# A decode step with a 4096-wide attention window: the first key loads over two queues, 256-byte key buffers, and a finer last cut

## The chip, the cores and the metric

The kernel runs on one core of one Trainium2 chip. The metric is the device time of one execution in microseconds (us); less is better. Names used below: PE is TensorE (matmuls; PEld its weight loads), DVE is VectorE, ACT is ScalarE, POOL is GpSimd, SP is SyncE, which only issues transfers here. PSUM is the memory that matmuls write to, SBUF the memory that the other engines and the transfers work on. A "q" behind an engine's name in the profile means its instruction queue (ACTq, SPq); q1 and q10 are the DMA queues that SP and ACT fill.

## The reference

One token (batch 1, one position, width 512) passes an attention over the last 4096 cached positions with 32 heads of 128, and beside it a small MLP block; the two are multiplied and added to the input.

```python
def reference(A_x, A_k_cache, A_v_cache, A_wq, A_wo, B_x, B_w1, B_w2, B_w3, B_w4):
    # attention on xn: W = 4096, 32 heads, Dh = 128
    q = (x @ wq).reshape(1, 1, 32, 128)
    k, v = k_cache[:, :, Sk - W:, :], v_cache[:, :, Sk - W:, :]
    p = softmax(einsum("bhqd,bhkd->bhqk", q, k) * Dh ** -0.5)
    s = einsum("bhqk,bhkd->bhqd", p, v) ... @ wo
    # block B on xn, with S = 1: the shifts leave only zeros, so hs = zeros @ w2
    x1 = x + hs
    g = silu(x1 + gelu(layernorm(x1) @ w3) @ w4)
    return A_x + s * g          # xn = layernorm(A_x) goes into both
```

The window's keys and values are 33.5 MB each in bf16, which with wq, wo and the block's weights makes the 79 MB that the core has to read.

## The kernel before

**Tiling.** The 32 heads are worked in eight groups of four (G = 4). A group's keys, or values, are one tile of 128 partitions by 128 chunks by 128 numbers in bf16 (4 MB, 32 KB per partition); each head has 32 of the partitions. Three key buffers (pool "k", K_BUFS = 3) and two value buffers (pool "v", V_BUFS = 2) are reused in turn. In this text K0 to K7 and V0 to V7 are the eight groups' keys and values.

**Scores.** The chunks of a group are shared between two ways. The first nd(g) chunks (64 in groups 0 and 7, else 80) go through DVE in four parts (k_vector): a product of keys and the query (L321, tile prod) and a sum along the 128 numbers (L323, tile S). The rest goes through PE in batches (k_turn, k_scores): transposes of two chunks at a time (L339), a copy by ACT from PSUM (L342, tile kt), and matmuls with the query (L350, tile sT). sm_own and sm_max bring both together and take the row maximum (L359, L364, L366); sm_turn and sm_exp spread the maximum over the partitions and take the exponentials (L372 to L388, tile pT).

**Values.** v_wide multiplies values with pT in matmuls over four chunks (L427, tile ov), v_turn and v_add fold the result (L444, L450), v_out divides (L471). Of the last group, the last 32 chunks go chunk by chunk through v_part (L461), into the same sum.

**Stages.** The main loop runs s = 0 to 9 with LAG = 2: stage s scores group s, takes the exponentials of group s - 1 and weighs the values of group s - 2. Inside it, the order on PE, DVE and ACT is the one written in the code (a manual schedule). What comes before the loop (layer norms, the query, the MLP block up to g_row, masks) is put in order by the scheduler, and so are its places among the first stage's instructions.

**Queues.** ACT issues x_bf, x_row and wq; every other load is issued by SP in program order through load(): w2, w3, w4 (two transfers), then K0 in two halves, K1, K2, V0, K3, V1 and so on. A load that reuses a buffer waits on SP until the engines are done with it, and what is behind it on SP waits too. V0's buffer lies in the memory of the pool "wts" (wq, w2, w3, w4 and a few tiles), which is closed in stage 2; V0's load waits for that pool's last readers, among them the matmuls into h2_ps (L155) that read hr.

**The end.** V7 comes in three pieces, cut at chunks 64 and 96 (cuts = (0, 64, 96, CP)); after it come two loads of the last four heads' rows of wo (wo_rows). When V7's last piece has landed, PE runs its 32 matmuls, DVE divides, PE multiplies with wo_rows (y_head), DVE multiplies with g_row and adds x, and SP writes the output.

**Memory.** The pool "k" is the first in SBUF; ahead of it lie 16,384 bytes of scratch and four constants of 32 bytes, so the key buffers begin at byte 16,512 of each partition. The value buffers begin at 160,000 and 192,768.

The lines that set the loads, and the names the change touches:

```python
kn = load_kv(k_pool, A_k_cache, s, (0, 64, CP) if s == 0 else (0, CP)) if s < NG else None   # L534
neg_half = const.tile([P, 33], FP32, name="neg_half")     # L121, only column 0 is read (L178)
bv = small.tile([P, P], FP32, name="bv")                  # L277
cuts = (0, 64, 96, CP)                                    # L526
```

Of the kernel before, what the change touches and what calls it, by code (L numbers as in the profile page):

```python
# [8 lines left out]
P = 128  # L9
BF16 = mybir.dt.bfloat16  # L10
FP32 = mybir.dt.float32
ACT = mybir.ActivationFunctionType
ALU = mybir.AluOpType
# [6 lines left out]
LAG = 2  # L20
# [6 lines left out]
def kernel(  # L27
# [14 lines left out]
    nc = tc.nc  # L42
# [3 lines left out]
    _, H, Sk, Dh = A_k_cache.shape  # L46
# [5 lines left out]
    CP = G * W // P  # L52
# [4 lines left out]
    scale = float(Dh) ** -0.5  # L57


    k_pool = ctx.enter_context(tc.tile_pool(name="k", bufs=K_BUFS))  # L60
    kt_pool = ctx.enter_context(tc.tile_pool(name="kt", bufs=4))
    prod_pool = ctx.enter_context(tc.tile_pool(name="prod", bufs=1))
    const = ctx.enter_context(tc.tile_pool(name="const", bufs=1))
    small = ctx.enter_context(tc.tile_pool(name="small", bufs=1))
# [7 lines left out]
    wts_guard = tc.tile_pool(name="wts", bufs=1)  # L72
    wts = wts_guard.__enter__()

    def load(dst, src):
        return tc.keep_in_program_order(nc.sync.dma_start(out=dst, in_=src))  # L76

    x_bf = small.tile([P, KC], BF16, name="x_bf")
    nc.scalar.dma_start(out=x_bf[:], in_=A_x.rearrange("a b (p c) -> p (a b c)", p=P))
# [5 lines left out]
                        in_=A_wq.rearrange("(a b c) n -> b a (c n)", a=4, c=KC))  # L85
# [6 lines left out]
    load(w4_sb[0:96, 10, :], B_w4[10 * P:F, :])  # L92


    def load_kv(pool, cache, g, cuts=(0, CP)):
        t = pool.tile([P, CP, Dh], BF16, tag="kv", name="kv")
        src = cache[0, G * g:G * g + G, W0:, :].rearrange("a (b c) d -> b a (c d)", b=PB)
        dst = t[:].rearrange("p c d -> p (c d)")
        for c0, c1 in zip(cuts, cuts[1:]):
            load(dst[:, c0 * Dh:c1 * Dh], src[:, :, c0 * Dh:c1 * Dh])  # L100
        return t

    ident_bf = const.tile([P, P], BF16, name="ident_bf")
    make_identity(nc, ident_bf[:])
# [13 lines left out]
    nc.vector.tensor_copy(out=sel[:], in_=ident_bf[:, 0:P:32].unsqueeze(1).to_broadcast([P, PB, G]))  # L118
    ind = const.tile([P, 1], FP32, name="ind")
    nc.vector.tensor_reduce(out=ind[:], in_=ident_f[:, 0:P:32], axis=AX.X, op=ALU.max)  # L120
    neg_half = const.tile([P, 33], FP32, name="neg_half")  # L121
    nc.vector.memset(neg_half[:], -0.5)


# [27 lines left out]
    def rows_add(ps, col, w, last):  # L152
        k = col.shape[0]
        for j in range(KC):
            nc.tensor.matmul(ps[32 * j:32 * j + 1, :], lhsT=col, rhs=w[0:k, j * P:(j + 1) * P],  # L155
                             start=False, stop=last, skip_group_check=True)
# [60 lines left out]
    for b in range(2):  # L217
# [5 lines left out]
        for t in range(2):  # L223
            rows = slice(64 * t, 64 * t + 64)
            nc.scalar.copy(out=q_pair[rows, 4 * b:4 * b + 4, :, G * t:G * t + G].rearrange("p g l a -> p g a l"),
                           in_=qt_ps[rows].bitcast(BF16).rearrange("p g (a m l) -> p g a m l", a=G, l=2)[:, :, :, 0, :])
# [14 lines left out]
    xn_row = small.tile([P, P], FP32, name="xn_row")  # L241
# [26 lines left out]
    for i, (col, w) in enumerate(terms):  # L268
# [5 lines left out]
    h2_ps = ps_misc.tile([P, P], FP32, tag="misc", name="h2_ps")  # L274
    rows_open(h2_ps)
    rows_add(h2_ps, ind, hr, True)
    bv = small.tile([P, P], FP32, name="bv")  # L277
    nc.vector.tensor_tensor(out=bv[:], in0=xn_row[:], in1=h2_ps[:], op=ALU.add)
    g_row = small.tile([P, P], FP32, name="g_row")
    nc.scalar.activation(out=g_row[:], in_=bv[:], func=ACT.Silu)  # L280


    make_masks(16)
# [13 lines left out]
                            op=ALU.max)  # L297
    par_t = const.tile([1 + G, PB, G], FP32, name="par_t")
    nc.vector.tensor_scalar(out=par_t[:],
                            in0=ident_f[0:1 + G, 1:1 + G].unsqueeze(1).to_broadcast([1 + G, PB, G]),  # L300
# [26 lines left out]
    def batches(g):  # L327
        n, m = nd(g), CP - nd(g)
        k = -(-m // 8)
        edges = [n + 2 * (m // 2 * i // k) for i in range(k + 1)]  # L330
        return list(zip(edges, edges[1:]))
# [12 lines left out]
    def k_scores(g, b):  # L344
        kt = kts.pop(b)
        c0, c1 = batches(g)[b]
        for i in range((c1 - c0) // 2):
            c = c0 + 2 * i - nd(g)
            for l in range(2):
                nc.tensor.matmul(st[g]["sT"][:, c:c + 2, :].rearrange("p c a -> p (c a)"),  # L350
                                 lhsT=kt[:, i, l::2], rhs=q_pair[:, g, l, :], start=(l == 0), stop=(l == 1))
# [55 lines left out]
    def load_wo(i):  # L407
        h0, n = blocks[i]
        load(wo_blk[i], A_wo[h0 * P:(h0 + n) * P, :].rearrange("(p t) n -> p t n", p=P))
# [4 lines left out]
    def load_rows(h, n):  # L414
        load(wo_rows[:, h - h_part:h - h_part + n, :],
             A_wo[h * P:(h + n) * P, :].rearrange("(h p) n -> p h n", p=P))
# [41 lines left out]
    def v_part(g, v, c0, c1):  # L458
        s = st[g]
        for c in range(c0, c1):  # L460
            nc.tensor.matmul(s["oT"][:], lhsT=v[:, c, :], rhs=s["pT"][:, c, :], start=False,  # L461
                             stop=(c == CP - 1), skip_group_check=True)
# [60 lines left out]
        rows_add(y_ps, o_blk[3][:, h - h_part:h - h_part + 1], wo_row(h), h == H - 1)  # L523

    NG = H // G
    cuts = (0, 64, 96, CP)  # L526
    region = tc.manual_schedule(engines={mybir.EngineType.PE, mybir.EngineType.DVE,
                                         mybir.EngineType.Activation})
    region.__enter__()
# [1 line left out]
    for s in range(NG + LAG):  # L531
        h = s - LAG
        last = h == NG - 1
        kn = load_kv(k_pool, A_k_cache, s, (0, 64, CP) if s == 0 else (0, CP)) if s < NG else None  # L534
        if s == LAG:
            wts_guard.__exit__(None, None, None)
            v_pool = ctx.enter_context(tc.tile_pool(name="v", bufs=V_BUFS))
            wo_blk[2] = v_pool.tile([P, 4, D], BF16, tag="wo_4", bufs=1, name="wo_4")
            wo_rows = v_pool.tile([P, H - h_part, D], BF16, tag="wo_rows", bufs=1, name="wo_rows")
        if last:  # L540
            v = load_kv(v_pool, A_v_cache, h, cuts)
            for r in (H - G, H - 2):
                load_rows(r, 2)
        elif h >= 0:
            v = load_kv(v_pool, A_v_cache, h)
        if h == 3:
            wo_24 = k_pool.tile([P, 32, D], BF16, tag="kv", name="wo_24")
            wo_blk[0], wo_blk[1] = wo_24[:, 0:16, :], wo_24[:, 16:24, :]
            load_wo(0)
        if h == 5:  # L550
            load_wo(1)
            load_wo(2)

        if s < NG:
            nb = len(batches(s))

            def keys(b0, b1):
                for b in range(b0, b1):
                    k_turn(s, kn, b)
                    if b > 0:  # L560
                        k_scores(s, b - 1)

            k_open(s)
            k_vector(s, kn, 0)
            keys(0, 2)
            if s == 7:
                v_turn(h - 1)
                v_add(h - 1)
                v_out(h - 1)
            elif s > 1:  # L570
                sm_den(s - 2)
                sm_rden(s - 2)
            elif s == 1:
                sm_max(0)
            k_vector(s, kn, 1)
            keys(2, 4)
            if s == 7:
                sm_den(h)
                sm_rden(h)
                keys(4, nb - 2)  # L580
                sm_turn(s - 1)
                keys(nb - 2, nb)
            else:
                if s > 0:
                    sm_turn(s - 1)
                keys(4, nb)
            k_scores(s, nb - 1)
            sm_own(s)
            if s == 7:
                k_vector(s, kn, 2)  # L590
                v_wide(h, v)
                sm_exp(s - 1)
                v_turn(h)
                y_open()
                k_vector(s, kn, 3)
                v_add(h)
                v_out(h)
                ox_spread(1)
                sm_max(s)
                continue  # L600
            if s > 0:
                sm_exp(s - 1)
            if h > 0:
                v_turn(h - 1)
            k_vector(s, kn, 2)
            if h >= 0:
                v_wide(h, v)
            if h > 0:
                v_add(h - 1)
                v_out(h - 1)  # L610
            if s == 6:
                ox_spread(0)
            k_vector(s, kn, 3)
            if s == 6:
                ox_pick(0)
            if s > 0:
                sm_max(s)
        elif s == NG:
            ox_pick(1)
            sm_turn(NG - 1)  # L620
            sm_exp(NG - 1)
            y_wide(1, False)
            sm_den(NG - 2)
            sm_rden(NG - 2)
            y_wide(0, False)
            warm(3)
            v_wide(h, v)
            sm_den(NG - 1)
            sm_rden(NG - 1)
            v_turn(h)  # L630
            v_add(h)
            v_out(h)
            ox_spread(2)
        else:
            v_open(h)
            warm(3)
            v_wide(h, v, cuts[1], last=False)
            ox_pick(2)
            y_wide(2, True)
            nc.scalar.copy(out=y_sum[:], in_=yr[0][:].rearrange("p j n -> p (j n)"))  # L640
            v_wide(h, v, cuts[2], cuts[1])
            v_turn(h)
            v_add(h)
            rows_add(y_ps, ind, y_sum, False)
            v_part(h, v, cuts[2], CP)
            v_out(h)
            for r in range(H - G, H):
                y_head(r)
# [36 lines left out]
```

## Time and profile before

| What | us |
|---|---|
| median of 3 runs (lowest, highest) | 193.31 (193.19, 193.39) |
| the profiled execution's own time | 193.34 |
| its span, first to last instruction | 191.2 |
| DVE busy | 150.9 (79%) |
| PE busy | 116.4 (61%) |
| ACT busy | 89.2 (47%) |
| DMA, mean over the span | 413 GB/s, 79.02 MB |
| one 4 MB key load, median from issue to landing | 31.3 |
| first key product on DVE starts | 26.09 |
| last piece of V7 landed | 186.33 |

The profile is of one execution. The span is shorter than the device time, which also counts what lies around the first and the last instruction. A row of the groups reads: line, engine, operation, tiles written and read with their shapes, count, busy time, mean time of one, and what ended the idle time ahead of it. A row of the timeline begins with the start time and the duration in us and ends, where the engine had been idle, with the idle time and what ended it in square brackets. A row of busy times by stretches has the stretch and its length, then busy us (and instructions) of PE, PEld, DVE, ACT and POOL, then PE's granted clock as a share of full speed, the mean busy share of the 16 DMA engines, and GB/s. A DMA queue's row has the number of packets, MB, and their time as a share of 16 engines.

The chain of work that ended last is, by the page, 46% DVE, 43% DMA, 5% PE and 3% ACT.

### The profile page before, as it was taken

Reading aid. Unit: us, or ns where it says so; the run is one execution under the profiler, and the core shown is the slowest. Engines: PE = TensorE matmul, PEld = TensorE weight load, DVE = VectorE, ACT = ScalarE, POOL = GpSimd, SP = SyncE. Lnnn points to the kernel's source line nnn. Section 1 sums busy time; section 2 is a strip of 40 time slices with the busy share of each in tenths; the row PEclk is TensorE's granted clock in tenths of the full one; section 3 lists DMA queues with packets and bytes.
Section 4 is the critical chain, followed back from the end, with each engine's and each line's share of the span. In section 5 each row is a group of like instructions: output and inputs, shape, how many; then the busy total and the mean of one; then the engine's idle time right before and its main releaser. Section 6 shows DMA issues by size and latency. Waiting matters only on the chain.

```text
span 191.2 us, 2839 instructions
## 1 busy us (share of the span) xinstructions
PE 116.4 (61%) x1159; PEld 74.2 (39%) x1159; DVE 150.9 (79%) x175; ACT 89.2 (47%) x191; POOL 2.3 (1%) x11
## 2 busy tenths in 40 slices
PE   1653754989825368256845772680888189739762
PEld 0430222767614334143334441540763077313322
DVE  1660159979999999999999999999999999980111
ACT  2001370888794076427464564542475148733120
POOL 2110000000000000000000000000000000000000
PEclk9999695555755557955695588557567858975998
DMA  6999999999999999999999999999999998999990
GB/s 211 447 430 404 431 418 439 439 439 437 432 434 439 432 429 432 432 439 432 422 432 432 418 422 418 452 439 435 439 432 434 435 432 372 471 425 405 420 371 32
DMA packets 4572, 79.02 MB, mean 413 GB/s; under 512 B 624, under 2 KB 1232, under 8 KB 1488
## 3 DMA queue, kind: packets, MB, share of 16 engines
q1 hardware_dynamic: 4264, 74.65, 91.6%
q10 hardware_dynamic: 296, 4.20, 5.1%
q8 instruction: 9, 0.15, 0.3%
q14 instruction: 3, 0.02, 0.0%
HBM read 78.84 MB, written 0.00 MB: 412 GB/s over the span
## 4 chain that ended last, share of the span: by engine, by line
DVE 46%; DMA 43%; PE 5%; ACT 3%; issue 1%; SPq 1%; ACTq 0%; DVEq 0%
DMA kv<-in_A_k_cache_dram 31%; DVE S L323 28%; DVE prod L321 15%; DMA kv<-in_A_v_cache_dram 10%; ACT kt L342 3%; DMA x_bf<-in_A_x_dram 2%; PE pt L339 2%; PE ov L427 1%; DVE m L366 1%; DVE S L364 1%; SPq L76 1%; PE sT L350 1%; DVE mx L374 1%; PE oT L461 1%; PE ot_ps L444 0%
## 5 line engine op out<-in xcount | busy, mean ns | idle before, releaser
L323 DVE TENSOR_REDUCE S<-prod 128x20 f32<-128x2560 bf16 (+1 forms) x32 | 86.0, 2686 | 1.1
L342 ACT COPY kt<-pt 128x1024 bf16<-128x1024 bf16 x52 | 51.2, 1013 | 40.4 <-PE pt L339 38.7
L339 PE MATMUL pt<-ident_f,kv 128*128 128x128 f32 x208 | 46.7, 376 | 10.8 <-DMA kv<-in_A_k_cache_dram 10.8
L321 DVE TENSOR_TENSOR prod<-kv,q_bc 128x2560 bf16<-128x2560 bf16 (+1 forms) x32 | 45.4, 1418 | 3.9 <-DMA kv<-in_A_k_cache_dram 3.7
L339 PEld LDWEIGHTS pt<-ident_f,kv 128*128 128x128 f32 x208 | 34.2, 196 | 14.4 <-DMA kv<-in_A_k_cache_dram 10.5
L350 PE MATMUL sT<-q_pair,kt 128*128 128x8 bf16 x416 | 19.4, 170 | 15.7 <-ACT kt L342 15.5
L350 PEld LDWEIGHTS <-kt 128*128 128x128 bf16 x416 | 16.4, 104 | 26.8 <-ACT kt L342 25.8
L427 PE MATMUL ov<-kv,pT 128*16 128x512 bf16 x248 | 22.0, 515 | 1.4 <-DMA kv<-in_A_v_cache_dram 1.4
L388 ACT ACTIVATE pT<-S,mb 128x128 bf16<-128x128 f32 x32 | 13.9, 573 | 0.3
L372 PE MATMUL mt_ps<-ident_f,m 128*1 128x128 f32 x8 | 2.9, 359 | 17.4 <-DVE rden L399 16.9
L433 ACT COPY ov_sb<-ov 128x512 f32<-128x512 f32 x8 | 4.7, 586 | 17.1 <-PE ov L427 17.1
L427 PEld LDWEIGHTS <-pT 128*16 128x16 bf16 x248 | 6.9, 109 | 13.2 <-issue 11.4
L359 ACT ACTIVATE own<-sT,par 128x48 f32<-128x48 f32 (+1 forms) x32 | 7.5, 356 | 3.7 <-PE sT L350 3.7
L444 PE MATMUL ot_ps<-ident_f,ov_sb 128*128 128x128 f32 x32 | 7.1, 359 | 2.9 <-ACT mb L384 1.9
L211 DVE CAST q_row<-qr_ps 128x512 bf16<-128x512 f32 x1 | 0.7, 692 | 9.9 <-PE qr_ps L208 9.9
L388 ACT ACTIVATION_READ_ACCUMULATOR pT<-S,mb 128x1 f32 x32 | 8.3, 258 | 0.0
L372 PEld LDWEIGHTS mt_ps<-ident_f,m 128*1 128x1 f32 x8 | 0.6, 80 | 17.9 <-DVE rden L399 17.2
L399 DVE RECIPROCAL rden<-den_ps 128x4 f32<-128x4 f32 x8 | 1.4, 175 | 7.0 <-PE den_ps L394 7.0
L381 PE MATMUL mb_ps<-md,par_t 5*128 5x4 f32 x16 | 3.9, 311 | 4.1 <-DVE md L376 4.1
L255 ACT ACTIVATE a_row<-a_ps 128x384 bf16<-128x384 f32 x1 | 0.5, 491 | 12.0 <-remote 12.0
L444 PEld LDWEIGHTS ot_ps<-ident_f,ov_sb 128*128 128x128 f32 x32 | 4.5, 178 | 3.9 <-ACT mb L384 2.3
L208 PE MATMUL qr_ps<-wq_sb,xq_bf 128*1 128x512 bf16 x32 | 3.1, 566 | 3.7 <-DMA wq_sb<-in_A_wq_dram 3.7
(122 smaller groups left out, 81.6 us busy)
## 6 DMA issues: line engine op xcount, KB each, us to landing
kv<-in_A_k_cache_dram SPq DMA_DIRECT2D x7, 4096.0 KB, 31.3
kv<-in_A_v_cache_dram SPq DMA_DIRECT2D x7, 4096.0 KB, 30.6
wq_sb<-in_A_wq_dram ACTq DMA_DIRECT2D x1, 4096.0 KB, 17.6
kv<-in_A_k_cache_dram SPq DMA_DIRECT2D x2, 2048.0 KB, 27.4
wo<-in_A_wo_dram SPq DMA_DIRECT2D x1, 2048.0 KB
kv<-in_A_v_cache_dram SPq DMA_DIRECT2D x1, 2048.0 KB
kv<-in_A_v_cache_dram SPq DMA_DIRECT2D x2, 1024.0 KB, 17.6
w_sb<-in_B_w_dram SPq DMA_DIRECT2D x1, 1376.0 KB, 9.1
```

The costliest lines, as they stand in the source:

```text
L321: nc.vector.tensor_tensor(out=prod[:, 0:m, :], in0=kn[:, rows, :], in1=q_bc[:, g:g + 1, :].to_broadcast([P, m, Dh]), op=ALU.mult)
L323: nc.vector.tensor_reduce(out=st[g]["S"][:, rows], in_=prod[:, 0:m, :], axis=AX.X, op=ALU.add)
L339: nc.tensor.transpose(pt[:, i, :], kn[:, c:c + 2, :].rearrange("p c d -> p (c d)").bitcast(FP32), ident_f[:])
L342: nc.scalar.copy(out=kts[b][:, 0:n, :], in_=pt[:, 0:n, :].bitcast(BF16))
L350: nc.tensor.matmul(st[g]["sT"][:, c:c + 2, :].rearrange("p c a -> p (c a)"), lhsT=kt[:, i, l::2], rhs=q_pair[:, g, l, :], start=(l == 0), ...
L359: nc.scalar.mul(s["own"][:, 0:m, a], s["sT"][:, 0:m, a], par[:, a:a + 1])
L372: nc.tensor.transpose(mt_ps[:], s["m1"][:], ident_f[:])
L381: nc.tensor.matmul(mb_ps[:], lhsT=par_t[:].rearrange("k b a -> k (b a)"), rhs=md[:], start=True, stop=True)
L388: nc.scalar.activation(out=s["pT"][:, :, a], in_=s["S"][:], func=ACT.Exp, scale=scale, bias=mb[:, a:a + 1], accum_out=s["sum"][:, a:a + 1])
L427: nc.tensor.matmul(ov[r:r + 4 * G], lhsT=s["pT"][:, c:c + 4, :].rearrange("p i a -> p (i a)"), rhs=v[:, c:c + 4, :], start=(i < 4), stop=( ...
L433: nc.scalar.copy(out=s["ov_sb"][:], in_=ov[:])
L444: nc.tensor.transpose(ot_ps[:, step * j:step * j + P], s["ov_sb"][:, j, :], ident_f[:])
```

## The change

Three parts.

1. **Key loads.** The loads of K0, K1 and K2 are moved ahead of the loop, right behind the weight loads, each as one transfer of 4 MB: K0 and K2 are issued by ACT, K1 by SP. load() and load_kv() get an engine argument for it. K0 is no longer loaded in two halves. From K3 on nothing changes.
2. **Placement.** neg_half moves from the pool "const" into a new pool "front" that is opened ahead of the key pool, with 32 columns instead of 33 (128 bytes per partition). The key buffers so begin at byte 16,640. bv gets 8 more columns that are neither written nor read; it makes up for the 32 bytes by which everything behind it would have moved, so that g_row and what comes after it, the value buffers too, stay where they were.
3. **The last cut.** The last 32 chunks of V7 are loaded as two pieces of 16 chunks, and v_part is called once for each.

```diff
+    front = ctx.enter_context(tc.tile_pool(name="front", bufs=1))
     k_pool = ctx.enter_context(tc.tile_pool(name="k", bufs=K_BUFS))
...
-    def load(dst, src):
-        return tc.keep_in_program_order(nc.sync.dma_start(out=dst, in_=src))
+    def load(dst, src, engine=None):
+        return tc.keep_in_program_order((engine or nc.sync).dma_start(out=dst, in_=src))
...
-    def load_kv(pool, cache, g, cuts=(0, CP)):
+    def load_kv(pool, cache, g, cuts=(0, CP), engine=None):
         t = pool.tile([P, CP, Dh], BF16, tag="kv", name="kv")
         src = cache[0, G * g:G * g + G, W0:, :].rearrange("a (b c) d -> b a (c d)", b=PB)
         dst = t[:].rearrange("p c d -> p (c d)")
         for c0, c1 in zip(cuts, cuts[1:]):
-            load(dst[:, c0 * Dh:c1 * Dh], src[:, :, c0 * Dh:c1 * Dh])
+            load(dst[:, c0 * Dh:c1 * Dh], src[:, :, c0 * Dh:c1 * Dh], engine)
         return t
+
+    early = [load_kv(k_pool, A_k_cache, g, engine=nc.sync if g == 1 else nc.scalar) for g in range(LAG + 1)]
...
-    neg_half = const.tile([P, 33], FP32, name="neg_half")
+    neg_half = front.tile([P, 32], FP32, name="neg_half")
...
-    bv = small.tile([P, P], FP32, name="bv")
-    nc.vector.tensor_tensor(out=bv[:], in0=xn_row[:], in1=h2_ps[:], op=ALU.add)
+    bv = small.tile([P, P + 8], FP32, name="bv")
+    nc.vector.tensor_tensor(out=bv[:, 0:P], in0=xn_row[:], in1=h2_ps[:], op=ALU.add)
     g_row = small.tile([P, P], FP32, name="g_row")
-    nc.scalar.activation(out=g_row[:], in_=bv[:], func=ACT.Silu)
+    nc.scalar.activation(out=g_row[:], in_=bv[:, 0:P], func=ACT.Silu)
...
-    cuts = (0, 64, 96, CP)
+    cuts = (0, 64, 96, 112, CP)
...
-        kn = load_kv(k_pool, A_k_cache, s, (0, 64, CP) if s == 0 else (0, CP)) if s < NG else None
+        kn = early[s] if s <= LAG else load_kv(k_pool, A_k_cache, s) if s < NG else None
...
-            v_part(h, v, cuts[2], CP)
+            v_part(h, v, cuts[2], cuts[3])
+            v_part(h, v, cuts[3], CP)
```

## The prediction

> **What bounds the kernel now.** I read the busy lines in 40 slices first, then busy time by stretches, then the timeline wherever a stretch begins or ends with a wait.
>
> ```profile
> DVE  1660159979999999999999999999999999980111
> DMA  6999999999999999999999999999999998999990
> ```
>
> Two resources are full at once: the 16 DMA engines from the second slice to the last but one, VectorE (DVE) from the ninth to the 35th. The stretches say how full.
>
> ```profile
> 41.90:60.00 18.10, 12.53 (x133) 10.40 (x133) 17.85 (x12) 14.88 (x29) 0.00 (x0) 0.59 1.01 433
> 60.00:130.00 70.00, 40.83 (x407) 25.91 (x406) 69.18 (x55) 35.44 (x87) 0.00 (x0) 0.66 1.01 433
> ```
>
> The third sum is DVE: 17.85 of 18.10 us and 69.18 of 70.00 us. The last two figures are the DMA share (1.01) and GB/s (433). Neither can give much, so I look for the slack of each.
>
> ```profile
> 26.09 1.23 DVE L321 TENSOR_TENSOR prod<-kv,q_bc 128x2048 bf16<-128x2048 bf16 x1 [2.19 <-DMA kv<-in_A_k_cache_dram]
> ...
> 32.23 1.94 PE L339 MATMUL pt<-ident_f,kv 128*128 128x128 f32 x8 [1.14 <-DMA kv<-in_A_k_cache_dram]
> ...
> 38.63 2.29 DVE L323 TENSOR_REDUCE S<-prod 128x16 f32<-128x2048 bf16 x1
> ...
> 41.91 1.49 DVE L321 TENSOR_TENSOR prod<-kv,q_bc 128x2560 bf16<-128x2560 bf16 x1 [0.99 <-DMA kv<-in_A_k_cache_dram]
> ...
> 134.17 1.49 DVE L321 TENSOR_TENSOR prod<-kv,q_bc 128x2560 bf16<-128x2560 bf16 x1 [0.55 <-DMA kv<-in_A_k_cache_dram]
> ...
> 181.50 1.04 PE L427 MATMUL ov<-kv,pT 128*16 128x512 bf16 x16 [1.02 <-DMA kv<-in_A_v_cache_dram]
> ...
> 183.93 0.61 PE L427 MATMUL ov<-kv,pT 128*16 128x512 bf16 x8 [0.41 <-DMA kv<-in_A_v_cache_dram]
> ...
> 186.38 0.96 PE L461 MATMUL oT<-pT,kv 128*128 128x4 bf16 x32 [0.17 <-DMA kv<-in_A_v_cache_dram]
> ```
>
> The first half of group 0's keys (K0) lets DVE start at 26.09; the second half lands at 32.2; DVE has finished K0 at 38.63 + 2.29 = 40.92 and waits 0.99 us for K1. From 41.91 to the last row maximum at 170.58 DVE waits for a transfer once more, 0.55 us for K6. Then TensorE (PE) runs the tail, and waits for the last values (V7) by 1.02, 0.41 and 0.17 us. So work that begins d late at K1 ends about d - 0.55 - 1.6 late: DVE is as critical as the DMA.
>
> **What the Trainium skill says.** "DMA: Bandwidth & Descriptors", section "Queues, rings and completion order": each DMA engine takes turns between the queues that have work for it, a packet from each. This trace agrees: between 12 and 17 us, with wq on ScalarE's queue (q10) and w4 on SP's (q1), both get the same number of packets, although one's are three times as large.
>
> ```profile
> q10 hardware_dynamic: 48, 1.57, 72.8%
> q1 hardware_dynamic: 48, 0.49, 23.1%
> ```
>
> The same page, "Issuing engines are not separate DMA queues": issuing from several engines saves only the issue time. The trace can't show a gain: one queue alone already fills the engines (1.01, 433 GB/s). The same page, "How a descriptor splits into AXI transactions": a descriptor that doesn't start at a multiple of 256 bytes pays for the bytes below its start. "VectorE: DVE Perf Modes", section "Mode 2x_1P": two bf16 results per cycle ask for 4-byte alignment only; the product's 2560 elements in 1.48 us are above one per cycle at that page's 0.96 GHz, so it has that mode already.
>
> **The change, part by part.**
>
> *Key loads.* Before, SP's queue holds w2, w3, w4, K0 in halves, K1, K2; ScalarE's holds wq. After, ScalarE's holds wq, K0, K2 and SP's the weights and K1. The bytes are the same and the engines are full, so only the order of landing changes. I count packets per engine from wq's end at about 19.2 us. SP has two or three 10 KB packets of w4, six of 1 KB (w4's last 96 rows over 16 engines) and two completions left: about eleven. ScalarE's queue then has K0's eight packets of 32 KB and two completions: about ten. Packet for packet, K0 gets nearly the whole bandwidth while the small ones are used up. K0 is therefore whole when K0 was whole before: 32.2 us. But DVE had half of it at 26.09; it starts 6.1 us later and takes 40.92 - 26.09 = 14.8 us, to 47.0.
>
> From about 30 us K1 (SP) and K2 (ScalarE) take turns, 8 packets each per engine, so both end near the time at which K2 ended before. V0, issued at 31.19 and landing 30.1 us later (61.3), came directly behind K2, and one 4.19 MB transfer at 433 GB/s takes 9.7 us: K2 landed at 51.6. By my count K1's packet follows K2's in each round, so K1 lands at 51.6; one packet earlier (32 KB at 27 GB/s, 1.2 us) if it leads. DVE begins K1 at max(47.0, 51.6) = 51.6 and not at 41.91: d = 9.7. The two bounds on d are 5.1 (K1 never waited for) and 14.2 (first rival).
>
> *What comes with it.* In the compiled order the scheduler puts a_bf (L260), hr (L273) and bv (L278) behind the first, second and third product of K0 on DVE, the h2 matmuls (L155) behind six of K0's eight transposing batches on PE, and the Gelu (L255) behind the q copies on ScalarE, with one more table load (1.28 us, the row at L255). Table load and Gelu lie between 25 and 28 us, where DVE and PE wait for K0 until 32.2: nothing. V0's load waits for h2, the last reader of the weights' pool: hr after two pairs (32.2 + 2 x 3.6 = 39.4), h2 by about 42. Before it was issued at 31.19. The queue is full with K1 and K2 to 51.6, so the 11 us are hidden; without that cover each microsecond would be DMA idle time. ScalarE's two new issues (0.5 us each; the second waits for w2, which lands 3.8 us after 0.73) hold up only the table load and the q copy of 21.84. K1's issue on SP waits for x_bf (4.7 us) and is used at 30.
>
> *Later loads.* All are issued 9.7 us later, as DVE and PE free the buffers later. The tightest is K6: 112.03 becomes 121.7, its first packet 1.0 us later (the first load is issued at 0.73, and the engines move nothing before 1.7), and the queue ahead of it ends about 123.5, one transfer and 0.9 us of completion before it landed at 134.1. It just holds. V7 (from 166.5 to 176) may leave the engines idle for 1 to 2 us, but by then the tail comes later than V7.
>
> *Alignment.* A 16 KB scratch and four constants of 32 bytes put the key buffers at 16,512, which is 128 above a multiple of 256; with neg_half in front they begin at 16,640, a multiple. Value buffers already lie at multiples. The trace's packets of 32 KB take 1213 ns in both, and a key and a value load both take 9.7 us, so I take 0. The page's price, at most 8 beats of 32 bytes on 32 KB, is an estimate of 0.8% of 9.7 us, under 0.1 us per load: bounds -0.6 and 0 for eight. For DVE I take 0 for the reason above, with -0.05 us per product as the lower bound (-1.4 for 28). bv's 8 added columns are never read and keep the later addresses; the 33rd column of neg_half was never read.
>
> *Last 32 chunks in two halves.* When V7's landing sets the end, 16 of 32 matmuls (0.48 of 0.96 us) move ahead of the last landing; but wo_rows, behind V7, land 18.5 us after an issue that ends at 169.5, near 187.6, where their matmuls run now. At most 0.2 us to gain. After the shift V7 is there before PE asks, so I take 0. One more issue on SP (0.55 us) delays wo_rows, which still land early.
>
> **Sum**, against the profiled execution's 193.34 us (span 191.2, and 2.1 around it; the median of the runs is 193.31, so the difference is nothing): 9.7 - 0.55 (K6 lands before DVE wants it) - 1.6 (V7 likewise) = 7.55, giving 200.9.
>
> **Rivals.**
> *A, the two queues share K0 and K1 evenly* (K0's packets come late, or w4's rest clears first). K0 then lands a packet before K1, about 40.6, DVE needs to 55.5 or 56.1, d = 14.2, time 193.34 + 14.2 - 2.15 = 205.4. For: both are queued by 6 us. Against: the equal packet counts above.
> *B, K1 isn't held up* (K2's packets come late): d = 47.0 - 41.9 = 5.1, time 196.3. Against: K2 is issued some 25 us before its turn.
> *C, the other side: aligned keys make DVE faster.* The products and reductions of K1 to K7, 28 pairs of 4.3 us (3.5 in K7), would have to save 7.5 us, 0.27 us each or 6%; from there on V7's landing sets the end again and the split tail takes 0.2: 193.1. For: the kernel is DVE-bound. Against: no row shows DVE depending on an address, and the reduction reads prod, not the keys.
> *D, nothing happens,* since the DMA sets the pace and DVE catches up: 193.3. Against: DVE has 0.55 us to catch up with in 128.
>
> **How the numbers follow.** Main case 0.77 (own range 199.4 to 202.4: K1 a packet earlier, DVE's bound, some waits of PE in K0), A 0.10, B 0.09, C 0.02, D 0.02. The range 198.0 to 203.8 holds the main case and the nearer parts of A and B. A measurement of this kernel tells 0.2% (0.4 us) from no change. Faster: C, 0.02; same: D, 0.02; slower: the rest, 0.96.
>
> **What would show it.** K0's first product near 32.3; the first of K1 near 51.6 behind a DMA wait of 4 to 5 us; no DVE wait for K6; no PE wait for V7 in the tail, and a DMA line that falls off before the end; equal packet counts of q1 and q10 between 31 and 50 us. A K0 product before 30 or after 36, DVE products shorter than 1.45 us, or idle DMA between 50 and 150 would make it wrong.

## The result, and the profile after

| | before | after |
|---|---|---|
| median, us (lowest, highest) | 193.39 (193.19, 193.69), 5 runs | 202.02 (201.12, 202.86), 5 runs |
| profiled execution, us; its span | 193.34; 191.2 | 202.02; 199.9 |
| first key product of K0, of K1, us | 26.09, 41.91 | 32.24, 51.56 |
| last row maximum on DVE ends, us | 170.58 | 180.40 |
| wide matmuls of V7's second piece begin on PE, us | 181.50 | 190.89 |

The ratio is 1.044, with an interval of 1.040 to 1.049: the changed kernel is 8.6 us slower. 200.9 was predicted, 1.1 us too little. Runs more than 1.5% above the fastest of their kernel are left out of every ratio in this text (three of e2's 22, one of e7's 22, one of e11's four).

The busy tenths of the page of after, in 40 slices of 5 us:

```profile
DVE  1650105976699999999999999999999999883011
DMA  6999999999999999999999998999999999949930
```

DVE is full from the twelfth slice on; before, from the tenth. It begins its steady run some 10 us later, and the whole full stretch has moved. The DMA line is full to slice 35, falls to 4 in the next one and ends early, where before it ran full almost to the end. Why DVE begins late is in its timeline (start and duration in us, operation, and in brackets the idle time before it with what ended it):

```profile
32.24 1.22 DVE L324 TENSOR_TENSOR prod<-kv,q_bc 128x2048 bf16<-128x2048 bf16 x1 [7.98 <-DMA kv<-in_A_k_cache_dram]
...
42.26 0.29 DVE L281 TENSOR_TENSOR bv<-xn_row,h_ps 128x128 f32<-128x128 f32 x1 [1.17 <-PE h_ps L158]
...
46.04 2.29 DVE L326 TENSOR_REDUCE S<-prod 128x16 f32<-128x2048 bf16 x1
...
51.56 1.49 DVE L324 TENSOR_TENSOR prod<-kv,q_bc 128x2560 bf16<-128x2560 bf16 x1 [3.23 <-DMA kv<-in_A_k_cache_dram]
```

DVE waits 7.98 us for K0 and starts on it at 32.24, works to 48.33, waits 3.23 us for K1 and starts on that at 51.56: 9.65 us later than before. From here on it waits for no transfer any more. The end, from PE's timeline:

```profile
185.38 1.46 PE L510 MATMUL wm<-zero_bf 128*128 128x512 bf16 x3
186.77 2.17 PE L430 MATMUL ov<-kv,pT 128*16 128x512 bf16 x32
...
190.89 1.04 PE L430 MATMUL ov<-kv,pT 128*16 128x512 bf16 x16
...
192.74 0.60 PE L430 MATMUL ov<-kv,pT 128*16 128x512 bf16 x8
...
195.07 0.94 PE L464 MATMUL oT<-pT,kv 128*128 128x4 bf16 x32
```

None of these rows has a wait for a transfer; before, the last three had 1.02, 0.41 and 0.17 us. Busy times by stretches of the same kernel (columns as before: PE, PEld, DVE, ACT, POOL, PE's granted clock, DMA share, GB/s):

```profile
170.00:180.00 10.00, 7.65 (x73) 4.34 (x73) 8.72 (x12) 5.92 (x17) 0.00 (x0) 0.64 0.73 297
180.00:190.00 10.00, 8.39 (x70) 3.23 (x70) 1.57 (x8) 2.59 (x12) 0.00 (x0) 0.66 0.98 387
```

The DMA engines stand at 0.73 between 170 and 180 us: V7 waits for its buffer and is issued from 177.7 us on. The bytes are the same as before (79.02 MB), but the end is now set by PE, not by the last transfer. The chain of waits of after says so too: 60% DVE, 25% DMA, 10% PE, against 46, 43 and 5% before.

### The profile page after: what moved, and what is told of

It reads as the page before. It is cut to its first block, busy times and chain, and to the rows that moved or that the text cites. A ratio compares the mean times of both kernels' runs of the same rounds, so it can differ in the third digit from the quotient of the medians.

```text
span 199.9 us, 2840 instructions
## 1 busy us (share of the span) xinstructions
PE 119.5 (60%) x1159; PEld 74.3 (37%) x1159; DVE 151.0 (76%) x175; ACT 90.2 (45%) x192; POOL 2.3 (1%) x11
## 2 busy tenths in 40 slices
DMA packets 4572, 79.02 MB, mean 395 GB/s; under 512 B 624, under 2 KB 1232, under 8 KB 1744
## 4 chain that ended last, share of the span: by engine, by line
DVE 60%; DMA 25%; PE 10%; ACT 1%; issue 1%; ACTq 0%; DVEq 0%
DVE S L326 36%; DMA kv<-in_A_k_cache_dram 23%; DVE prod L324 18%; PE ov L430 3%; DMA x_bf<-in_A_x_dram 2%; PE yr_ps L521 2%; DVE S L367 1%; DVE m L369 1%; PE wm L510 1%; PE ot_ps L447 1%; PE pt L342 1%; DVE mx L377 1%; ACT ov_sb L436 1%; DVE md L379 1%; ACT kt L345 1%
## 5 line engine op out<-in xcount | busy, mean ns | idle before, releaser
L342 PE MATMUL pt<-ident_f,kv 128*128 128x128 f32 x208 | 45.4, 366 | 8.2 <-DMA kv<-in_A_k_cache_dram 8.2
L342 PEld LDWEIGHTS pt<-ident_f,kv 128*128 128x128 f32 x208 | 33.3, 191 | 12.3 <-issue 8.5
L430 PE MATMUL ov<-kv,pT 128*16 128x512 bf16 x248 | 23.9, 551 | 0.0
L213 ACT CAST q_row<-qr_ps 128x512 bf16<-128x512 f32 x1 | 0.6, 585 | 15.5 <-PE qr_ps L211 15.5
L384 PEld LDWEIGHTS mb_ps<-md,par_t 5*128 5x128 f32 x16 | 3.8, 290 | 7.1 <-PE sT L353 4.6
```

What stands on the lines that cost most here:

```text
L342: nc.tensor.transpose(pt[:, i, :], kn[:, c:c + 2, :].rearrange("p c d -> p (c d)").bitcast(FP32), ident_f[:])
L384: nc.tensor.matmul(mb_ps[:], lhsT=par_t[:].rearrange("k b a -> k (b a)"), rhs=md[:], start=True, stop=True)
L430: nc.tensor.matmul(ov[r:r + 4 * G], lhsT=s["pT"][:, c:c + 4, :].rearrange("p i a -> p (i a)"), rhs=v[:, c:c + 4, :], start=(i < 4), stop=( ...
```

## The experiments

The theory at this point: all of the loss comes from when K0 and K1 land. K0 as one transfer gives DVE nothing until the whole of it is there, and K2, on the other queue, takes every second packet from K1. The rivals: the placement or the finer cut has a part in it; the queues share K0 and K1 in another way; or the end has a loss of its own.

**The three parts alone**

*e1, the key loads alone* (placement and cut as before).

> The three key loads moved as in the change; key buffers where they were (byte 16,512), last cut as before. Theory (the landing order of K0, K1, K2 is the whole loss): 202.0, K0's first product at 32.2, K1's at 51.6, a ratio to before of 1.04 to 1.05. Rival (placement or the finer cut has a share of at least 0.4 us in the 8.6): under 201 or over 203.

202.90 us (202.09 to 203.31), ratio 1.048 (1.046 to 1.050). DVE's timeline of it:

```profile
32.26 1.22 DVE L323 TENSOR_TENSOR prod<-kv,q_bc 128x2048 bf16<-128x2048 bf16 x1 [8.04 <-DMA kv<-in_A_k_cache_dram]
...
51.70 1.49 DVE L323 TENSOR_TENSOR prod<-kv,q_bc 128x2560 bf16<-128x2560 bf16 x1 [2.88 <-DMA kv<-in_A_k_cache_dram]
```

Both starts lie within 0.15 us of those in the changed kernel, behind nearly the same waits (7.98 and 3.23 us there): the key loads alone bring the whole loss. The median is even 0.9 us above the changed kernel's, though the ranges overlap. In the two profiles that difference arises at the end: the last row maximum ends 0.5 us later (180.90), and the 32 wide matmuls take 2.77 us instead of 2.17.

*e2, the placement alone.* neg_half in its own pool ahead of the keys, bv with 8 more columns, all else as before.

> Only neg_half in front and bv wider: key buffers at a multiple of 256 bytes, loads and cuts as before. Theory (placement is worth nothing): ratio 1.000 within 0.001, packets of key loads and products on DVE as long as before (1.48 us for 128x2560). Rival C of the prediction (aligned keys make DVE or the DMA faster): 0.2 to 0.6 us faster than before, as V7's landing then bounds the end.

193.26 us, ratio 0.999 (0.998 to 1.000). Key buffers at a multiple of 256 bytes make neither DVE nor the transfers measurably faster: the product of 2560 elements takes 1.48 us in both profiles, and both move 433 GB/s between 60 and 130 us. Rival C, which needed 7.5 us from this, is out.

*e3, the finer cut alone.*

```diff
-    cuts = (0, 64, 96, CP)
+    cuts = (0, 64, 96, 112, CP)
...
-            v_part(h, v, cuts[2], CP)
+            v_part(h, v, cuts[2], cuts[3])
+            v_part(h, v, cuts[3], CP)
```

> Only the last 32 chunks in two pieces. Theory (wo_rows, which land after V7, leave at most 0.2 us to gain): 0 to 0.2 us faster, ratio 0.999 to 1.000; in the trace 16 instead of 32 matmuls of L461 after V7's last piece, and the y_ps matmuls not earlier than wo_rows' landing near 187.6. Rival (the last landing alone sets the end): 0.45 us faster.

193.65 us, ratio 1.001 (1.0002 to 1.0017): 0.2 us slower where a gain of up to 0.2 was expected. In its trace the 32 matmuls of L461 begin at 186.10 without a wait (before: 186.38, after 0.17 us), but the 16 matmuls with wo_rows behind them take 0.62 us instead of 0.39, and most of the gain is gone. Whether the added issue ahead of wo_rows is the cause was not settled; it is at the limit of what can be measured.

**The key loads taken apart**

*e7, all three early loads on SP's queue, K0 in two halves* (the changed kernel, with the queues and the halves of before).

```diff
-    early = [load_kv(k_pool, A_k_cache, g, engine=nc.sync if g == 1 else nc.scalar) for g in range(LAG + 1)]
+    early = [load_kv(k_pool, A_k_cache, g, (0, 64, CP) if g == 0 else (0, CP)) for g in range(LAG + 1)]
```

> The change with all three key loads on SP's queue and K0 in halves: placement, the early place in the program and the finer cut stay. Theory: nothing is left of the loss, ratio 0.999 to 1.001, K0's first product at 26.1, K1's at 41.9. Rival (the early place in the program reorders other work and costs by itself): over 194.

193.55 us, ratio 1.0005 (0.9994 to 1.0017).

```profile
25.93 1.23 DVE L324 TENSOR_TENSOR prod<-kv,q_bc 128x2048 bf16<-128x2048 bf16 x1 [1.80 <-DMA kv<-in_A_k_cache_dram]
...
41.90 1.49 DVE L324 TENSOR_TENSOR prod<-kv,q_bc 128x2560 bf16<-128x2560 bf16 x1 [1.14 <-DMA kv<-in_A_k_cache_dram]
```

Placement, finer cut and the loads' place ahead of the loop are all still in it, and nothing of the loss is. What costs is the queues and the lost halves, and only these.

*e5, the kernel before with K0 loaded whole on SP's queue.*

```diff
-        kn = load_kv(k_pool, A_k_cache, s, (0, 64, CP) if s == 0 else (0, CP)) if s < NG else None
+        kn = load_kv(k_pool, A_k_cache, s) if s < NG else None
```

> Before, with K0 as one load; all key loads on SP's queue. Theory: K0 whole at 32.2, K1 at 41.8 as before; DVE needs 14.1 us for K0 (a_bf, hr, bv ahead of it) and starts K1 near 46.3: d = 4.4, so 195.6 to 196.8 (loss d - 2.15 if the tail is as in the sum, d - 1.05 if it is as the changed kernel showed). Rival (the halves are worth nothing, DVE catches up): 193.4.

197.21 us (196.93 to 198.22), ratio 1.020 (1.017 to 1.023), above the 195.6 to 196.8 expected.

```profile
32.38 1.22 DVE L321 TENSOR_TENSOR prod<-kv,q_bc 128x2048 bf16<-128x2048 bf16 x1 [4.35 <-DMA kv<-in_A_k_cache_dram]
...
46.70 1.49 DVE L321 TENSOR_TENSOR prod<-kv,q_bc 128x2560 bf16<-128x2560 bf16 x1
```

K1's first product follows without a wait, 4.8 us later than before: that is what the lost halves alone cost at K1.

*e6, the changed kernel with K2 on SP's queue behind K1,* so that only K0 goes through ACT's.

```diff
-    early = [load_kv(k_pool, A_k_cache, g, engine=nc.sync if g == 1 else nc.scalar) for g in range(LAG + 1)]
+    early = [load_kv(k_pool, A_k_cache, g, engine=nc.scalar if g == 0 else nc.sync) for g in range(LAG + 1)]
```

> The change with K2 behind K1 on SP's queue; only K0 on ScalarE's. Theory: K0 at 32.2 as in the change, and K1, with nothing to take turns with, near 41.8; DVE ends K0 near 48.3 (16.1 us, as in the changed kernel) and starts K1 there without a wait: d = 6.4, 197.7 to 198.8. So K2's queue alone is worth 3.2 to 4 us of the 8.6. Rival (two queues, not the order, cost the time): 201 to 202.

199.04 us (198.53 to 199.98), ratio 1.029 (1.026 to 1.032), a little above the 197.7 to 198.8 expected. K0 again at 32.34, and now:

```profile
48.90 1.49 DVE L324 TENSOR_TENSOR prod<-kv,q_bc 128x2560 bf16<-128x2560 bf16 x1
```

No bracket: K1 is there. It is the changed kernel's wait of 3.23 us that is gone, and 3.0 us of its time with it. So K2 on the other queue, taking packets from K1, is what held K1 up. This is rival B made to happen. K1 starts 2.2 us later than in e5 because the MLP's a_bf, hr and bv, with a wait of 1.61 us for h_ps, stand between K0's products on DVE; in e5 they come before K0.

*e4, the changed kernel with K0 in halves,* queues as changed.

```diff
-    early = [load_kv(k_pool, A_k_cache, g, engine=nc.sync if g == 1 else nc.scalar) for g in range(LAG + 1)]
+    early = [load_kv(k_pool, A_k_cache, g, (0, 64, CP) if g == 0 else (0, CP),
+                     engine=nc.sync if g == 1 else nc.scalar) for g in range(LAG + 1)]
```

> The change with K0 in two halves again, both on ScalarE's queue. Theory (queues take turns packet by packet, whatever a packet's size): K0's first half lands near 26, its second half of 8 packets of 16 KB now stands against K1's packets of 32 KB and lands near 40.6 instead of 32.2; K1 lands near 41.9 and not at 51.6. DVE is done with K0 near 48 and starts K1 there: d = 6.2, 197.4 to 198.5. Rival 1 (K1 is late because of K2, however K0 is cut): K1 at 51.6, 202. Rival 2 (the engines share by bytes or in order of issue): second half near 32 and K1 near 42, 193.4.

207.88 us (207.09 to 208.12), ratio 1.074 (1.072 to 1.076): far from every expectation, and slower than the change itself. Its timeline, DVE and then PE:

```profile
25.93 1.23 DVE L325 TENSOR_TENSOR prod<-kv,q_bc 128x2048 bf16<-128x2048 bf16 x1 [1.70 <-ACT q_bc L220]
...
46.63 0.69 DVE L277 COPY hr<-hr_ps 128x512 f32<-128x512 f32 x1 [13.58 <-PE hr_ps L274]
...
56.24 1.49 DVE L325 TENSOR_TENSOR prod<-kv,q_bc 128x2560 bf16<-128x2560 bf16 x1
...
41.85 1.97 PE L343 MATMUL pt<-ident_f,kv 128*128 128x128 f32 x8 [13.26 <-DMA kv<-in_A_k_cache_dram]
```

The first half is there at 25.93, and K1 isn't waited for, as was thought. But with 16 KB packets against K1's 32 KB the second half was only there at 41.8 us. PE needs it for its transposes, and in the compiled order hr_ps's matmuls stand behind the first of these. DVE needs hr_ps before its third product. So DVE stood 13.58 us for a transfer that it doesn't itself read, through PE's order.

*e9, e4 with the order mended*: masks and constants moved up, and the MLP's end (a_row to g_row) put into the written-out order ahead of the loop.

```diff
+    region = tc.manual_schedule(engines={mybir.EngineType.PE, mybir.EngineType.DVE,
+                                         mybir.EngineType.Activation})
+    region.__enter__()
     a_row = wts.tile([P, 3, P], BF16, name="a_row")
...
-    region = tc.manual_schedule(engines={mybir.EngineType.PE, mybir.EngineType.DVE,
-                                         mybir.EngineType.Activation})
-    region.__enter__()
     v_pool = None
```

> The kernel with group 0's keys in two halves on ScalarE's queue (207.88 us), with the MLP's end (Gelu, a_bf, hr, h2, bv) put into the written-out order ahead of group 0's products. Theory: the time beyond the transfers came from hr, a DVE instruction behind K0's second pair, whose matmuls stood on PE behind the transposes of K0's late second half. Freed of that, DVE does two pairs from about 32 us, waits for K0's second half until 41.8, has K0 done at 49.0 and doesn't wait for K1: d is 7.1 instead of 14.3, the time 207.9 - 7.2 = 200.7, less what group 7's stage no longer waits; 198.2 to 200.9. Rival: PE's late transposes or K1's landing hold DVE in any case: 205 to 208 as before.

200.12 us (199.44 to 201.41), ratio 1.035 (1.030 to 1.040): within the expectation, 7.8 us faster than e4, so the order behind PE's late transposes is shown to be where 7.8 of e4's 14.5 us went. The way is not quite the one expected:

```profile
46.29 1.49 DVE L330 TENSOR_TENSOR prod<-kv,q_bc 128x2560 bf16<-128x2560 bf16 x1
...
53.87 0.42 DVE L373 TENSOR_REDUCE S<-own 128x64 f32<-128x256 f32 x1 [3.24 <-ACT own L368]
```

DVE's 64 chunks of K0 all lie in the first half, so it went through K0 without the expected wait and began K1 at 46.29. Then it waited 3.24 us for the scores of the other half, which PE had begun on only at 41.65, when it landed. The late half is paid either way, but at 3.2 us and not at 13.6.

**The MLP's end**

*e10, e6 with the MLP's end ahead of K0, as in e9.*

> K0 whole on ScalarE's queue, K1 and K2 on SP's (199.04 us), with the MLP's end ahead of group 0's products. Theory: that kernel was slower than the one with K0 whole on SP's queue (197.21) because a_bf, hr, bv and the wait for h2's matmuls stand between K0's products: 2.2 us. With them ahead K1 begins at 46.7 and not at 48.9, and the time is 196.6 to 197.6. Rival: the difference came from the queues: 198.5 to 199.5.

199.63 us (198.71 to 200.96), ratio 1.033 (1.027 to 1.039): not faster than e6; the theory as put failed. PE's timeline says why:

```profile
32.21 0.59 PE L301 MATMUL hr_ps<-w_sb,a_bf 96*1 96x512 bf16 x1 [0.89 <-DMA w_sb<-in_B_w_dram]
```

The last matmul into hr_ps waits for w4's last 96 rows. They come in 1 KB packets on SP's queue, each of which waits its turn behind one of K0's 32 KB packets, and land only when K0 does. hr is then at 32.83, bv at 34.44, K0 starts at 34.65 and K1 at 48.96, as late as in e6. The 2.2 us can't be had by the order while K0 comes through the other queue.

*e11, the changed kernel with the MLP's end ahead of K0.*

> The changed kernel with the MLP's end ahead of group 0's products. Theory: K0 is done 1.3 to 1.6 us earlier, but K1 lands at 51.6 in both, so DVE waits that much longer for it: no difference, 201.3 to 202.7 as the changed kernel. Rival: K0's stage is on the path after all: 200.3 to 200.8.

202.36 us (201.79 to 202.36, and one run of 205.13 left out), ratio 1.045 (1.043 to 1.048), the changed kernel's time.

```profile
51.42 1.49 DVE L329 TENSOR_TENSOR prod<-kv,q_bc 128x2560 bf16<-128x2560 bf16 x1 [1.47 <-DMA kv<-in_A_k_cache_dram]
```

Here w4's rest was waited for until 33.24, K0 started at 35.68 and was done at 49.96. K1's wait shrank from 3.23 to 1.47 us and K1 began where it did. What is lost inside K0's stage costs nothing as long as K1 lands at 51.5. But the expectation that K0 would be done earlier was wrong, for the same reason as in e10.

**The end**

*e8, the changed kernel without the three matmuls on zeros (wm, L510) ahead of the last wide group.*

```diff
             y_wide(0, False)
-            warm(3)
```

> The change without the three filler matmuls (warm) ahead of v_wide of group 6; the output is the same. The prediction was 1.1 us short; in the trace these fillers take 1.46 us (1.07 before) and v_wide 2.17 (1.90). Theory (the tail is bound by PE, whose slower clock there made up about 0.7 us of the 1.1): 0.6 to 1.5 us faster than the changed kernel, 200.5 to 201.4. Rival 1 (V7's later landing bounds the tail): no difference. Rival 2 (without the fillers the clock drops for longer): slower than 202.5.

202.13 us (201.63 to 202.69), ratio 1.044 (1.042 to 1.047): no difference, where 0.6 to 1.5 us less had been expected. It isn't V7 either, as that rival had it: no row of PE in this end waits for a transfer. The wide matmuls begin 0.7 us earlier than in the changed kernel, and take longer:

```profile
186.06 3.54 PE L430 MATMUL ov<-kv,pT 128*16 128x512 bf16 x32
```

3.54 us instead of 2.17. The granted clock was 0.53 between 180 and 190 us, against 0.66, and this execution was already 0.8 us behind at the last row maximum (181.23 against 180.40). In these profiles the three matmuls gave back what they took, so they aren't a cost of the end that can be removed. Since the granted clock differs from one execution to the next (means of 0.689 to 0.726 in the five of the changed kernel), one pair of profiles does not show that they raise it.

No run was measurably faster than the kernel before, and none of the findings points to a version that would be: in the kernel before the DMA engines are full from the second slice to the last but one.

## Why the prediction came out right, and what it missed

**When K0 lands.** Predicted whole at 32.2, used at 32.24. The packets on the two queues between 19.2 and 30 us, counted in the trace of after (packets, MB, share of 16 engines):

```profile
q10 hardware_dynamic: 145, 4.23, 90.9%
q1 hardware_dynamic: 137, 0.42, 9.5%
```

Nearly the same number of packets, ten times the bytes: K0 got nine tenths of the engines while SP's queue had w4's small rows. This agrees with what the Trainium skill states ("DMA: Bandwidth & Descriptors", section "Queues, rings and completion order"), that an engine takes turns between its queues by the packet, and it is why rival A did not happen.

**When K1 lands.** Predicted 51.6, used at 51.56; d = 9.65 instead of 9.7. The reason was that K2 shares the engines with K1, and e6 shows it. The equal packet counts foretold between 31 and 50 us seem not to have come out:

```profile
q1 hardware_dynamic: 163, 4.69, 57.1%
q10 hardware_dynamic: 129, 3.70, 45.3%
```

But at 4.69 MB SP's queue had moved more than the 4.19 MB of K1; what is above that is the first of V0, which stands behind K1 on that queue and has the engines to itself once K2 is through. With the stretch ended at 48 us the counts are nearly equal, and the bytes are:

```profile
q10 hardware_dynamic: 114, 3.67, 50.1%
q1 hardware_dynamic: 117, 3.67, 50.0%
```

So K1 and K2 did march in step, half of the engines each, and neither was whole before both nearly were. The foretold sign came out; only its stretch was drawn 2 us too long.

**K0's stage.** 14.8 us was taken for DVE's way through K0; it was 16.1 (32.24 to 48.33). The 14.8 us were read from the kernel before, where hr and bv already lay between K0's products. What is new there is a_bf (0.16 us) and the wait for h_ps (1.17 us): the sum left both out, and together they are the difference. It cost nothing, but only because K1 was later still: its wait shrank to 3.23 us instead of the 4 to 5 us foretold. e6 shows the price where K1 isn't late.

**Placement, cut, V0, later loads.** Placement is nothing (e2), as costed. The cut was costed at nothing to a gain of 0.2, and is 0.2 slower alone (e3). V0's issue moved to 42.30, foretold "by about 42", and hid behind K1 and K2. K6 was issued at 121.67 (121.7 foretold), and no wait for it is left. V7's late issue leaves the engines idle, as foretold (2.7 us of the ten from 170 us on, where 1 to 2 were said), and PE never waits for it.

**The mis-sized term: what the end gives back.** The sum took off 0.55 for K6 and 1.6 for V7. DVE took back the first by waiting for PE: its last row maximum ends 9.82 us late where 9.65 - 0.55 = 9.10 was due, since the stage of group 7 now has two waits for PE, of 0.61 us (ot_ps; none before) and 0.46 us (mt_ps; 0.36 before). And of the 1.6 us only 1.1 came: the span grew by 8.7, 1.12 less than 9.82. The matmuls on zeros took 1.46 us instead of 1.07, and the wide ones behind them 2.17 instead of 1.90. In the stage of group 7 the 32 wide matmuls took longer too (the first row is of before, the second of after):

```profile
164.60 1.90 PE L427 MATMUL ov<-kv,pT 128*16 128x512 bf16 x32
...
174.39 3.23 PE L430 MATMUL ov<-kv,pT 128*16 128x512 bf16 x32
```

PE's granted clock was 0.96 there before (160 to 170 us) and 0.64 after (170 to 180 us). A slow PE alone need not cost anything. In e3, which starts on time, these 32 took 3.31 us, and the last row maximum still ended only 0.12 us later than before; the matmuls on zeros and the wide ones of the end took 1.46 and 2.21 us, and used up the wait for V7's second piece (1.02 us before, none in e3), while the output row still began at 188.30 (188.36 before). Where no wait for V7 is left, such a delay moves the end. Taking K1's start in each trace and the prediction's own rule (193.34 + d - 2.15) shows that the gap has the same sign in every kernel listed:

| | K1 starts, us | d | by the rule, us | measured median, us | gap |
|---|---|---|---|---|---|
| e5 | 46.70 | 4.79 | 195.98 | 197.21 | 1.2 |
| e6 | 48.90 | 6.99 | 198.18 | 199.04 | 0.9 |
| e10 | 48.96 | 7.05 | 198.24 | 199.63 | 1.4 |
| after | 51.56 | 9.65 | 200.84 | 202.02 | 1.2 |
| e1 | 51.70 | 9.79 | 200.98 | 202.90 | 1.9 |
| e4 | 56.24 | 14.33 | 205.52 | 207.88 | 2.4 |

(e9 is left out, since its wait comes after K1's start; e8 and e11 start K1 as the changed kernel does and take its time.) With the time of the profiled execution itself in place of the median, the gaps run from 1.2 (e5) to 2.1 us (e1). So the start is carried through, and the end gives back 1.0 us in the changed kernel and at most 1.3 in the others, instead of 2.15. How much of the gap is the clock and how much PE's work in another order beside DVE was not separated; e8 only shows that the matmuls on zeros are not it.

## What to carry to other kernels

A second queue brought no bandwidth here, where one already filled the engines (a share of 1.01 before; 50.1% and 50.0% for the two queues after); it only changed what landed first. So ask for each stage which transfer it waits for, and keep a transfer that is needed later (here K2) from sharing with one that is needed now (K1). A first load in pieces is worth the pieces where an engine can begin on the first one, but look at which engine reads which piece and at what stands behind the late one in that engine's order: in e4 that cost 7.8 us. When an end that was waiting for a transfer no longer waits, don't take the whole of that wait as gain: delays of the engine's own can have been hidden in it, as in e3.

## What the runs showed of the hardware that was not expected

- A small transfer can be held back by a large one on another queue, packet by packet: w4's last 96 rows (1 KB packets) were waited for until 33.24 us in e11, where K0 and K2 follow each other on ACT's queue in 32 KB packets, and until 32.21 in e10, where K0 is alone there. In e9, where K0 comes in 16 KB packets, the matmuls that read them ran from 29.26 us without a wait.
- The same 32 wide matmuls on PE took 1.90 us in the end of the kernel before, 2.17 in after and 3.54 in e8, where the granted clock, averaged over the ten microseconds around them, was 0.70, 0.66 and 0.53. That the clock alone makes the difference is not shown.
